# Four input places, solves on POOL and four-quadrant products in a recurrence with two feed-forward networks

## The chip, the cores and the metric

One core of one Trainium2 chip runs the program. Inputs are laid out by the host beforehand. The metric is the device time of one execution in microseconds (us).

## What is computed

The input has 4 batches x 8 heads (32 states), 768 steps and a head dimension of 40. Each head carries a 40 x 40 state:

```python
for t in range(S):
    y[:, :, t] = np.einsum('bhd,bhde->bhe', rt, state)
    Sa = np.einsum('bhde,bhe->bhd', state, at)
    state = state * wt[:, :, None, :] - np.einsum('bhd,bhe->bhde', Sa, bt) + np.einsum('bhd,bhe->bhde', vt, kt)
x = y.transpose(0, 2, 1, 3).reshape(B * S, H * D)   # 3072 x 320
h = x @ w_in                                         # 320 x 2048
g = np.where(h >= 1, h, np.where(h <= -1, 0.0, (h + 1) ** 2 / 4))
x = g @ w_out                                        # 2048 x 320
out = ((x @ w_a) * (x @ w_b)) @ w_out2               # 320 x 1536, 1536 x 320
```

The network weights arrive as 64-bit floats; the kernel turns them into 32-bit ones itself.

## The kernel before

**Chunks.** The 768 steps are cut into 24 chunks of 32; four chunks make a block. Within a chunk the recurrence is turned into small matrix products for each of the 32 states (16 pairs, two states of a pair on different partitions) and one triangular system per state.

**Preparation** (`prepare`, L118) of a chunk reads one 104 x 2065 tile, `ein`, loaded by `load_e` (L115). DVE scans the decays (L128, L131), POOL copies `wc` (L129) and sets `cre` (L127), DVE writes `lab` (L137), POOL scales k and b (L139; DVE for chunks 0 and 1), TensorE makes the products `pab` (L146, 64 columns each), and after them SP issues the next `ein` load into the same buffer. DVE masks the product into `lab` (L152), and ACT's queue writes a part of it, `amd`, to DRAM (L154). `p1_stage` (L158) does the same kind of scaling for a whole block (`ptw`, `pkb`, results `pwd` and `wtd` in DRAM).

**Solve.** The triangular systems are inverted by elimination on the whole block, 128 systems on 128 partitions: `solve` (L200) has 60 DVE instructions, each needing the one before (L209, L211). For the first block, `solve_pair` (L218) does two chunks at a time, with each system's rows split over two partitions, in 62 instructions (L236, L238), closed by a POOL selection (L241). The input `apm` is loaded from `amd`, the result goes to `xtd` in DRAM, and `load_xt` (L261) brings it back as `xtl`.

**The recurrence** (`core`, L284) of a chunk: `pw` (L295) multiplies `lab` and the state tile `ru`; ACT negates it into `ws` (L297); `pu` (L303) multiplies by the solved `xtl`; ACT copies it into `ru` (L306); `pss` (L314) gives the next state, which DVE scales (L317); then transposes `put` and `pst` (L325, L332). `outp` (L338) makes the outputs with `pg` (L344) and `py` (L355); `x_out` (L366) transposes them into `xa` for the first network. `pw` and `pu` write two quarters of 32 partitions each, 64 of 128 in all; `py` writes four quarters of 32.

**Order.** The program first drains preparations 0 and 1, the first solve, the first block stage, preparations 2 and 3, the second solve, and then all of `conv`, the conversion of the first network's weights, at a priority 300 places back. Then it walks through 26 slots. A slot g holds `core(g)`, `outp(g - 1)`, `x_out(g - 2)`, the preparations given to it (two a slot at first, then one), a share of the block stage and of the solve of a later block (the solve of block n in slots 4n - 2 and 4n - 1), and 16 steps of the first network (from slot 3 on) at a priority 8000 places back. A network block has 256 rows and takes some 33 steps, so half a block falls to a slot; what is left runs after the last slot. From slot 12 on the second network's weights are converted. A planner places instructions on each engine by priority and by its own costs, and each engine then works in that fixed order.

**Conversion.** `from_f64` (L489) uses four DVE instructions, two on ACT and one product on POOL for a tile, then ACT copies the high part and DVE or POOL subtracts (`SE`, two of three on DVE). `stage` gives one of two staging places; the loads are issued by SP.

**Networks.** The first network (`ffn1_half`, L616) has products `pha` and `ya`, DVE and ACT for the activation (L629 to L634), and POOL for the remainder `gl` (L636). The second (`Second`, L657) runs after all of it, block by block.

## Time and profile before

| what | us |
|---|---|
| median of 3 runs | 1578.63 |
| lowest, highest | 1574.61, 1583.82 |
| the profiled execution | 1573.97 |
| its span in the profile | 1572.3 |

Rows of a timeline give the start in us, the length in us, engine, line, operation, tiles and shapes, a count of like instructions that follow one another, and in brackets the idle time of the engine before them with what ended it. PE is TensorE's matmul, PEld its weight load, SPq the queue of SP. In the table by stretches each engine has its busy time and instructions, then come the granted TensorE clock as a share of full speed, the busy share of the 16 DMA engines, and their rate. TensorE's clock has two levels, 1.2 and 2.4 GHz; a share between 0.5 and 1 is a mean of both. A product of 32-bit floats stands as two matmul records.

### The profile page before, as it was taken

The numbers are of one execution on the slowest core, as the hardware profiler recorded it, in microseconds if no ns is written. First come the engines' busy times: TensorE is split into PE (matmuls) and PEld (weight loads), VectorE is DVE, ScalarE is ACT, GpSimd is POOL, SyncE is SP. The second block draws the span as 40 slices with busy tenths as digits, with TensorE's granted clock in tenths as the row PEclk, the third lists the DMA queues.
The fourth block names the chain that finished last, engine by engine and source line by source line (L and its number), as shares of the span: only waits on it lengthen the run. The fifth ranks groups of instructions, "written<-read, shape, count | busy, mean of one in ns | idle before, by whom it ended". The sixth has DMA issues, their size and how long they took to land.

```text
span 1572.3 us, 36942 instructions
## 1 busy us (share of the span) xinstructions
PE 1220.9 (78%) x15602; PEld 1099.9 (70%) x15602; DVE 829.0 (53%) x1690; ACT 537.3 (34%) x1193; POOL 473.7 (30%) x523
## 2 busy tenths in 40 slices
PE   0010233577798998988899998978999999999996
PEld 0010232566688887877789987877888888888885
DVE  6579587883584585458557737787421111111110
ACT  1213324123123333333343545666432222222221
POOL 7135433312112323221322223455422222222221
PEclk9999996556579878788899988999999999999999
DMA  5846677777534334343433334443110000100000
GB/s 131 185 106 159 127 154 161 169 151 158 123 101 113 93 83 108 96 104 94 114 93 87 105 102 126 129 141 100 41 49 21 18 20 18 37 1 17 1 18 19
DMA packets 193987, 144.34 MB, mean 92 GB/s; under 512 B 139028, under 2 KB 168724, under 8 KB 191316
## 3 DMA queue, kind: packets, MB, share of 16 engines
q1 hardware_dynamic: 168468, 138.74, 35.4%
q10 hardware_dynamic: 25344, 3.15, 1.5%
q8 instruction: 124, 2.03, 0.5%
q14 instruction: 51, 0.42, 0.1%
HBM read 111.97 MB, written 29.88 MB: 90 GB/s over the span
## 4 chain that ended last, share of the span: by engine, by line
PE 45%; DMA 6%; DVE 6%; issue 2%; ACT 1%; POOL 1%; SPq 0%; DVEq 0%; ACTq 0%; POOLq 0%
PE pb L582 9%; PE pa L582 7%; PE po L582 7%; PE ya L582 5%; PE pha L582 4%; DMA ein<-in_ein_dram 3%; PE pg L344 2%; PE ya L574 1%; PE pa L574 1%; PE pab L146 1%; PE pha L574 1%; PE pw L295 1%; PE pss L314 1%; PE pu L303 1%; PE put L325 1%
## 5 line engine op out<-in xcount | busy, mean ns | idle before, releaser
L636 POOL TENSOR_TENSOR gl<-cl,gh 128x256 fp32r<-128x256 f32 x192 | 152.5, 796 | 333.7 <-ACT gh L634 223.8
L683 DVE TENSOR_TENSOR gf<-pb,asb 128x512 f32<-128x512 f32 x72 | 49.8, 692 | 308.4 <-PE pb L582 308.4
L582 PE MATMUL pha<-xa,wi 128*128 128x256 f32 x1239 | 195.0, 301 | 0.0
L146 PE MATMUL pab<-lab,ein 40*64 40x32 f32 x1536 | 80.0, 259 | 143.0 <-POOL ein L139 75.9
L687 POOL TENSOR_TENSOR gl<-gf,gh 128x512 fp32r<-128x512 f32 x72 | 92.8, 1289 | 310.8 <-ACT gh L685 310.8
L582 PEld LDWEIGHTS pha<-xa,wi 128*128 128x128 f32 x1239 | 179.3, 211 | 0.0
L146 PEld LDWEIGHTS pab<-lab,ein 40*64 40x64 f32 x1536 | 71.0, 179 | 149.6 <-POOL ein L139 92.9
L582 PE MATMUL ya<-wo,gh 128*128 128x320 f32 x576 | 143.4, 331 | 5.1 <-ACT yo L892 5.1
L630 ACT ACTIVATE cl<-cl 128x256 f32<-128x256 f32 x192 | 80.1, 417 | 157.8 <-DVE cl L629 152.1
L502 POOL TENSOR_TENSOR cvf<-cvf,cve 128x256 f32<-128x256 f32 (+2 forms) x84 | 79.2, 943 | 128.3 <-DVE cve L500 74.4
L582 PE MATMUL ya<-wo,gl 128*128 128x320 f32 x384 | 115.0, 336 | 1.5 <-POOL gl L636 1.2
L303 PE MATMUL pu<-ws,xtl 32*32 32x40 f32 x1536 | 47.6, 226 | 83.2 <-DMA xtl<-xtd 72.2
L582 PEld LDWEIGHTS ya<-wo,gh 128*128 128x128 f32 x576 | 107.1, 208 | 5.9 <-ACT yo L892 5.6
L634 ACT CAST gh<-cl 128x256 fp32r<-128x256 f32 x192 | 77.6, 404 | 98.3 <-DVE cl L632 90.7
L582 PE MATMUL po<-wo,gh 128*128 128x320 f32 x504 | 108.5, 309 | 0.0
L629 DVE TENSOR_SCALAR cl<-pha 128x256 f32<-128x256 f32 x177 | 73.9, 417 | 62.5 <-PE pha L582 55.8
L303 PEld LDWEIGHTS pu<-ws,xtl 32*32 32x32 f32 x1536 | 40.9, 130 | 91.0 <-issue 76.5
L574 PE MATMUL pha<-xa,wi 128*128 128x256 f32 x177 | 61.1, 345 | 45.8 <-DVE cl L632 45.8
L632 DVE TENSOR_TENSOR cl<-pha,cl 128x256 f32<-128x256 f32 x177 | 74.1, 419 | 40.0 <-ACT cl L630 38.5
L685 ACT CAST gh<-gf 128x512 fp32r<-128x512 f32 x72 | 44.7, 620 | 138.2 <-DVE gf L683 138.2
L582 PE MATMUL pb<-wo,w 128*128 128x512 f32 x288 | 90.8, 397 | 0.0
L582 PE MATMUL pb<-wi,w 128*128 128x512 f32 x288 | 90.8, 396 | 0.0
(147 smaller groups left out, 2683.3 us busy)
## 6 DMA issues: line engine op xcount, KB each, us to landing
ein<-in_ein_dram SPq DMA_DIRECT2D x24, 838.9 KB
vut<-in_vtin_dram SPq DMA_DIRECT2D x24, 416.0 KB
raw<-in_moe_w_out_dram SPq DMA_DIRECT2D x28, 320.0 KB
pkb<-in_pin_dram SPq DMA_DIRECT2D x12, 640.0 KB
ru<-in_vin_dram SPq DMA_DIRECT2D x48, 160.0 KB
pwd<-pkb SPq DMA_DIRECT2D x12, 640.0 KB
kbi<-pwd SPq DMA_DIRECT2D x48, 160.0 KB
lg<-pwd SPq DMA_DIRECT2D x48, 160.0 KB
```

The costliest lines, as they stand in the source:

```text
L146: nc.tensor.matmul(pab[FR[p]:FR[p] + 64, j, :], lhsT=kb[o:o + D, j, :], rhs=lab[o:o + D, p, j, :], start=True, stop=True)
L303: nc.tensor.matmul(pu[UR[p]:UR[p] + C, j, :], lhsT=xt[o:o + C, hs.start + j, :], rhs=ws[o:o + C, hs.start + j, :], start=True, stop=True)
L502: nc.gpsimd.tensor_tensor(out=f, in0=f, in1=e.bitcast(F32), op=ALU.mult)
L574: nc.tensor.matmul(**products[0])
L582: nc.tensor.matmul(**p)
L629: nc.vector.tensor_scalar(out=cl, in0=ph, scalar1=-1.0, scalar2=1.0, op0=ALU.max, op1=ALU.min)
L630: nc.scalar.activation(out=cl, in_=cl, func=AF.Square, scale=0.5, bias=0.5)
L632: nc.vector.tensor_tensor(out=gf, in0=ph, in1=cl, op=ALU.max)
L634: nc.scalar.copy(out=gh, in_=gf)
L636: nc.gpsimd.tensor_tensor(out=gl, in0=gf, in1=gh.bitcast(F32), op=ALU.subtract)
L683: nc.vector.tensor_tensor(out=gf, in0=pb, in1=asb, op=ALU.mult)
L687: nc.gpsimd.tensor_tensor(out=gl, in0=gf, in1=gh.bitcast(F32), op=ALU.subtract)
```

## The change

It does these things:

- The inputs `ein` of chunks 0 to 3 get four places (three of them in tiles that later hold network weights); chunk 4 and later ones use the first place. All block-0 inputs of `p1_stage` get their own places too.
- Setting up memory: `cre`, `crp` are cleared by DVE, `kbi` is copied by ACT; the copy `wc` and the setting of `cre` move from POOL to DVE; the scaling of k and b moves to POOL for all but chunk 0, and that of `pkb` for the first block.
- `solve` runs on POOL instead of DVE. The first block's first half is solved on DVE, the second half on POOL, with its own tiles; both come after all four preparations.
- `pab` and `pg` are made in groups of 32 columns, two products in place of one of 64 columns. `pw` and `pu` write all four quarters of 32 partitions at once, in one bank instead of two; `ws` is one ACT instruction instead of two; `amd`, `xtd` and `xtl` have a layout for it, and `xtl` is one load on 128 partitions, with two tiles.
- The conversion of the first network's weights goes 900 places back instead of 300; its loads are issued by ACT; for the first 20 units there are six staging places instead of two (four of them in the two `xa` tiles). One of three subtractions is left on DVE (`SE`).

```diff
-            EIN = pre.tile([128, LE], F32, name="ein")
+            EIN = [pre.tile([128, LE], F32, name="ein")] + [spare(n, F32)[:, 0:LE] for n in ("wi3", "wo3", "wi2")]
...
-                nc.sync.dma_start(out=EIN[0:104], in_=ein[g])
+                nc.sync.dma_start(out=EIN[g if g < 4 else 0][0:104], in_=ein[g])
...
-                nc.gpsimd.memset(cr[:, 0:NEW - 1:SEG], 1.0)
+                nc.vector.memset(cr[:, 0:NEW - 1:SEG], 1.0)
...
-                nc.gpsimd.tensor_copy(out=wc, in_=wx[:, C::SEG])
+                nc.vector.tensor_copy(out=wc, in_=wx[:, C::SEG])
...
-                eng = nc.vector if g < 2 else nc.gpsimd
+                eng = nc.gpsimd if g else nc.vector
...
-                            nc.tensor.matmul(pab[FR[p]:FR[p] + 64, j, :], lhsT=kb[o:o + D, j, :],
-                                             rhs=lab[o:o + D, p, j, :], start=True, stop=True)
+                            for n in range(2):
+                                f = FR[p] + C * n
+                                nc.tensor.matmul(pab[f:f + C, j, :], lhsT=kb[o:o + D, j, n, :],
+                                                 rhs=lab[o:o + D, p, j, :], start=True, stop=True)
                     yield
-                if g + 1 < NCH:
+                if g == 0:
+                    load_e(4)
+                elif 4 <= g < NCH - 1:
                     load_e(g + 1)
...
-                    nc.vector.tensor_tensor(out=tv, in0=X[:, 0:m, m:m + 1].to_broadcast([128, m, n]),
+                    nc.gpsimd.tensor_tensor(out=tv, in0=X[:, 0:m, m:m + 1].to_broadcast([128, m, n]),
...
-                    nc.vector.tensor_tensor(out=X[:, 0:m, m + 1:], in0=X[:, 0:m, m + 1:], in1=tv, op=ALU.add)
+                    nc.gpsimd.tensor_tensor(out=X[:, 0:m, m + 1:], in0=X[:, 0:m, m + 1:], in1=tv, op=ALU.add)
...
-                    t = XT[g] = mid.tile([128, NC_, C], F32, name="xtl")
-                    for p in range(2):
-                        nc.sync.dma_start(out=t[XR[p]:XR[p] + C], in_=xtd[g // 4][g % 4, p].rearrange("k s t -> s k t"))
+                    t = XT[g] = mid.tile([128, HC, C], F32, name="xtl", bufs=2)
+                    nc.sync.dma_start(out=t, in_=xtd[g // 4][g % 4].rearrange("k q s t -> (q s) k t"))
...
+                quads = [(C * (2 * h + p), p, h) for h in range(2) for p in range(2)]
+                pw = bank("pw", [128, HC, D])
+                for j in range(HC):
+                    for q, p, h in quads:
+                        nc.tensor.matmul(pw[q:q + C, j, :], lhsT=lab[:, p, 2 * j + h, :],
+                                         rhs=ru[:, p, 2 * j + h, :], start=True, stop=True)
+                ws = mid.tile([128, HC, D], F32, name="ws")
+                nc.scalar.activation(out=ws, in_=pw, func=AF.Copy, scale=-1.0)
+                yield
+                pu = bank("pu", [128, HC, D])
+                for j in range(HC):
+                    for q, p, h in quads:
+                        nc.tensor.matmul(pu[q:q + C, j, :], lhsT=xt[q:q + C, j, :], rhs=ws[q:q + C, j, :],
+                                         start=True, stop=True)
+                for q, p, h in quads:
+                    nc.scalar.copy(out=ru[UR[p]:UR[p] + C, p, h::2], in_=pu[q:q + C])
...
             drain(prepare(0))
             drain(prepare(1))
-            drain(solve_pair(0))
             drain(p0)
+            drain(prepare(2))
+            drain(prepare(3))
+            drain(solve_pair(0, nc.vector))
             load_kb(0, KBI)
             load_kb(0, LG)
             load_wt(0)
-            drain(prepare(2))
-            drain(prepare(3))
-            drain(solve_pair(2))
-            with tc.high_priority(offset=-300):
-                for _ in conv:
-                    pass
+            drain(solve_pair(1, nc.gpsimd))
+            with tc.high_priority(offset=-900):
+                more = [xap.tile([128, 6, 256], F32R, name="xa").bitcast(U32).rearrange("p j t -> p (j t)") for _ in range(2)]
+                extra.extend(t[:, 640 * i:640 * i + 640].rearrange("p (n w) -> p n w", w=2) for t in more for i in range(2))
+                QS["raw"] = 'A'
+                for n, _ in enumerate(conv):
+                    if n == 20:
+                        extra.clear()
+                QS["raw"] = 'S'
...
-    SE = 'DDP'
+    SE = 'PPD'
```

## Rows read from the trace of the kernel before

**Rows 1.** Busy time by stretches (us from the span's start), all engines.
```profile
0.00:186.00 186.00, 16.78 (x320) 16.21 (x320) 126.19 (x226) 48.36 (x90) 84.40 (x84) 1.00 0.63 142
...
283.00:482.00 199.00, 151.84 (x2884) 136.69 (x2883) 138.08 (x245) 52.59 (x109) 40.73 (x43) 0.60 0.60 137
482.00:787.00 305.00, 269.73 (x4499) 246.24 (x4499) 188.70 (x408) 106.55 (x259) 83.41 (x108) 0.83 0.39 99
787.00:997.00 210.00, 198.83 (x3640) 182.87 (x3635) 129.50 (x311) 100.04 (x249) 60.66 (x86) 0.93 0.39 104
997.00:1122.00 125.00, 109.50 (x1172) 100.91 (x1167) 94.98 (x223) 77.37 (x199) 64.54 (x80) 1.00 0.37 107
1122.00:1572.00 450.00, 433.82 (x2293) 379.73 (x2291) 75.47 (x124) 119.85 (x222) 105.39 (x89) 0.99 0.07 22
```

**Rows 2.** Timeline of PE: products pu and pw of chunks 0, 4, 8, 16, 23.
```profile
186.51 0.44 PE L303 MATMUL pu<-ws,xtl 32*32 32x40 f32 x4 [66.70 <-DMA xtl<-xtd]
...
364.81 1.45 PE L303 MATMUL pu<-ws,xtl 32*32 32x40 f32 x27 [5.48 <-DMA xtl<-xtd]
...
483.41 0.77 PE L295 MATMUL pw<-ru,lab 128*32 128x40 f32 x32
...
786.70 0.77 PE L295 MATMUL pw<-ru,lab 128*32 128x40 f32 x32
...
996.44 0.77 PE L295 MATMUL pw<-ru,lab 128*32 128x40 f32 x32
```

**Rows 3.** Timeline of SP's queue, 60 to 180 us.
```profile
63.27 2.54 SPq L116 DMA_DIRECT2D ein<-in_ein_dram  x1
...
76.42 0.55 SPq L226 DMA_DIRECT2D apm<-amd  x1
...
163.86 5.02 SPq L244 DMA_DIRECT2D xtd<-apm  x2
...
172.19 4.74 SPq L265 DMA_DIRECT2D xtl<-xtd  x2
```

**Rows 4.** Timeline of DVE: first solve.
```profile
96.61 0.19 DVE L236 TENSOR_TENSOR tm<-apm 128x31 f32<-128x31 f32 x1 [9.35 <-POOL apm L230]
...
120.98 3.60 DVE L238 TENSOR_TENSOR apm<-apm,tm 128x126 f32<-128x126 f32 x1
```

**Rows 5.** Timeline of POOL beside it.
```profile
120.85 3.58 POOL L184 TENSOR_TENSOR pkb<-pkb,ptw 128x1280 f32<-128x1280 f32 x1 [1.09 <-DMA pkb<-in_pin_dram]
...
162.63 0.83 POOL L241 TENSOR_SCALAR_AFFINE_SELECT apm<-apm 128x512 f32<-128x512 f32 x1 [1.01 <-DVE apm L238]
```

**Rows 6.** Tile apm: count, ns min/median/max, first and last start, forms.
```profile
L209 DVE TENSOR_TENSOR tm<-apm x150: 166/368/3570, 298.9 to 883.5; 128x30 f32<-128x30 f32 x10, 128x58 f32<-128x58 f32 x10, 128x84 f32<-128x84 f32 x10, 128x108 f32<-128x108 f32 x10
...
L236 DVE TENSOR_TENSOR tm<-apm x62: 168/272/2536, 96.6 to 256.6; 128x126 f32<-128x126 f32 x6, 128x30 f32<-128x30 f32 x4, 128x56 f32<-128x56 f32 x4, 128x78 f32<-128x78 f32 x4
```

**Rows 7.** Groups by line and form on POOL: busy us, mean ns | idle before.
```profile
L636 POOL TENSOR_TENSOR gl<-cl,gh 128x256 fp32r<-128x256 f32 x192 | 152.5, 796 | 333.7 <-ACT gh L634 223.8 <-issue 59.3 <-PE pha L582 9.4
```

**Rows 8.** DMA from 0 to 482 us: total, and the loads of pkb.
```profile
DMA packets 122575, 69.12 MB, mean 143 GB/s; under 512 B 104907, under 2 KB 110923, under 8 KB 120971
...
pkb<-in_pin_dram SPq DMA_DIRECT2D x12, 640.0 KB
```

**Rows 9.** Timeline of PE: small products at either clock level.
```profile
682.22 0.80 PE L355 MATMUL py<-lg,rg 128*32 128x40 f32 x64
...
686.54 1.47 PE L146 MATMUL pab<-lab,ein 40*64 40x32 f32 x44
...
279.97 3.63 PE L146 MATMUL pab<-lab,ein 40*64 40x32 f32 x64 [16.12 <-DMA pkb<-in_pin_dram]
```

**Rows 10.** One wait for ein: chain of waits, then timelines of DVE and PE.
```profile
689.22 7.16 DMA ein<-in_ein_dram
...
696.41 1.26 DVE L128 TENSOR_TENSOR_SCAN ewx<-ein,cre 104x529 f32<-104x529 f32 x1 [5.02 <-DMA ein<-in_ein_dram]
...
698.04 0.58 PE L574 MATMUL pha<-xa,wi 128*128 128x256 f32 x1 [4.60 <-DVE cl L632]
```

More of the change, by code (lines that the diff above doesn't have):

```diff
@@ L42, in rwkv_moe_kernel @@
     wtd = [dram.tile([C, 4, NP // 2, 2, D], F32, name=f"wtd{i}") for i in range(NSB)]
-    amd = [dram.tile([4, 2, NP // 2, C, C], F32, name=f"amd{i}") for i in range(NSB)]
-    xtd = [dram.tile([4, 2, NP // 2, C, C], F32, name=f"xtd{i}") for i in range(NSB)]
+    amd, xtd = ([dram.tile([4, NP // 4, 4, C, C], F32, name=f"{n}{i}") for i in range(NSB)] for n in ("amd", "xtd"))
     const = ctx.enter_context(tc.tile_pool(name="const", bufs=1))
@@ L243, in solve_pair @@
                 for h in range(2):
-                    qu('xs').dma_start(out=xtd[sb][c:c + 2].rearrange("c p k (j h) t -> h (c p k) j t", h=2)[h, :, ::-1],
+                    nc.sync.dma_start(out=xtd[0][2 * i:2 * i + 2].rearrange("c k q (j h) t -> h (c k q) j t", h=2)[h, :, ::-1],
                                       in_=X[64 * h:64 * h + 64])
-                mark["solve", g] = last(DVE)
                 yield
@@ L286, in core @@
                 ru, nxt, lab, wc = RU[g % 2], RU[(g + 1) % 2], LAB[g % PL], WC[g % (PL + 1)]
[L287 removed]
+                if g % 4 == 0 or g == 2:
                     load_xt(g)
                 xt = XT.pop(g)
[L290 to L298 removed]
@@ L894, in ffn_block, with spare @@
             yield
-        step, conv2 = recurrence(ffn_block, wk, units1(stg, wa, WI, WO), lambda: units2(NE), early())
+        def spare(name, dtype):
+            return wa.tile([128, 2560], dtype, name=name)
+        step, conv2 = recurrence(ffn_block, wk, spare, units1(stg, wa, WI, WO), lambda: units2(NE), early())
         wo = w2s.enter_context(tc.tile_pool(name="wo2", bufs=1, side="right", reuse_waits="tile"))
```

103 lines of the change are left out of this document (46 added, 57 removed).

## The prediction

> **What bounds the kernel now.** I read the table by stages first, then followed the first late product backwards through the queues. In [rows 1] the last stage, 1122 to 1572, is TensorE at the higher clock level almost throughout (433.8 of 450 us, clock 0.99); the diff touches nothing there, so those 450 us stay. The first 186 us hold 16.8 us of TensorE work, with DVE at 126 us and the DMA engines at 0.63; from 283 to 482 TensorE runs at a mean clock of 0.60, that is mostly at 1.2 GHz. From 482 to 787 it is busy 270 of 305 us at 0.83. So there are two places to gain: the start, and the product stream between 283 and 997.
>
> The start is one chain. The first correction product (pu of chunk 0) begins at 186.51 after TensorE idled 66.70 us for the solved matrices [rows 2]. Backwards [rows 3 to 5]: xtl is loaded at 172.19, xtd written at 163.86, the solve's last step on POOL stands at 162.63, its first product on DVE at 96.61, its load (apm) was issued at 76.42, and at 63.27 the single ein buffer was only being filled for the third chunk. The solve took 66 us for 62 instructions whose median is 0.27 us [rows 6]: DVE did conversions and preparation between them, and was held by POOL, as at 120.98, where an addition of 126 elements took 3.60 us while POOL multiplied pkb for 3.58 us [rows 4, 5].
>
> The marks for pace are the starts of pu in chunks 0 and 4, 186.5 and 364.8, and of pw in chunks 8, 16 and 23, 483.4, 786.7 and 996.4 [rows 2]: some 37 us a chunk up to chunk 8, 38 from 8 to 16, 30 after that.
>
> **The front, up to chunk 8.** *Inputs.* With four places the loads of chunks 0 to 3 are issued at once. By the shapes, four ein are 4 x 104 x 2065 x 4 B = 3.4 MB, pin 2.0 MB, v, vt and r 1.2 MB, and six staged weight tiles about 1.7 MB on ACT's queue beside them: 8.3 MB, at the 142 GB/s of the first stage [rows 1] 58 us. The apm load of chunks 0 and 1 queues behind most of it, so its data are there at about 57 us, where now the first product starts at 96.6: 39 us earlier. *First solve.* 62 instructions at 0.27 us are 17 us [rows 6], now 66; chunks 2 and 3, the block scans and POOL's own second solve lie beside it, so I take 30, nearer the floor because conversions are put back by 900 places and not by 300. *From the last step to pu* it is 23.9 us now (162.63 to 186.51); one xtl load instead of two and a shorter SP queue, but the last step stands in POOL's queue among the second solve's: I take 20. Sum 57 + 30 + 20 = 107, so 80 us earlier; bounds 88 (57 + 17 + 14, the last from 172.19 on) and 147 (57 + 66 + 24).
>
> *Chunks 0 to 8.* Chunk 0 to 4 takes 178 us now. Its bound is the serial round of the one ein place (chunks 4 to 7 still use it), then the solve of the second block. The load of chunk 4 now starts early, which saves at most one round; the solve moves to POOL: 60 instructions of 30 to 240 elements. No row has POOL doing this. From below it costs DVE's 0.37 us each [rows 6], 22 us; from above the 0.80 us of POOL's 256-element subtraction [rows 7], 48 us. I take 0.6, 36 us, nearer that row because the largest steps have its size; DVE's row is stretched by conflicts too, so the chain is about even. I take 10 us less for chunks 0 to 4 and 5 less for 4 to 8 out of 119. Chunk 8 then starts at 107 + 168 + 114 = 389. *Can DMA follow?* By 482 us 69.1 MB have moved, all twelve pkb loads among them [rows 8], so the last three of six blocks (3 x 3.9 MB by shapes) are ahead of need: 57 MB are needed, at 142 GB/s 404 us. I take the gain at chunk 8 as 95 us (388); bounds 45 (the first solve's ceiling, and the rest unchanged) and 140 (its floor, with 42 us off the two stretches).
>
> **Small products.** py, 32 columns in four quadrants, takes 0.80 us for 64 records, 12.5 ns each; pw in two quadrants 0.77 us for 32, 24 ns [rows 2]; pab with 64 columns 1.47 for 44, 33 ns; at 1.2 GHz pab takes 3.63 for 64, 57 ns [rows 9]. A pw or pu of 64 records falls from 1.54 to 0.80 us, 0.74 less each; pab and pg double to 128 records but at 12.5 ns are 1.60 instead of 2.14, 0.54 less each. Sum 2.55 us a chunk at the higher level, about 1.7 times that, 4.4, at the lower (57 / 33). At the mean clock 0.83 of 482 to 787 a third of the time is at the lower level: 3.2 x 8 = 25 us; from chunk 16 on, mostly without pab (2.55 - 0.54, and a little at the lower level), 2.2 x 7 = 16. Sum 41. It counts only where TensorE is on the path. Every preparation still ends in a wait: the ein load takes 7.16 us, DVE's scan idles 5.02 us for it, TensorE then 4.60 us [rows 10], and nothing in the diff removes this after chunk 3. So the lower bound of this term is 0; the upper is 64, four us a chunk, if the clock falls less often.
>
> The Trainium skill, TensorE: Matmul & The Clock Gate, Part 3, says that a weight load runs beside matmuls in flight only when its row group differs. By that rule pw, with all 128 rows, would gain nothing from four column groups, and pab and pg would pay for twice the loads; py's row speaks against it. What this would make of the sum is the third rival.
>
> **Edits with little on the path.** *Solves of blocks 2 to 5 on POOL* add about 36 us each to a POOL that is busy 83 of 305 us; DVE loses 22. The subtraction gl of the first network waits behind one solve step at a time, under 1 us, and pab's multiplication on POOL too; DVE's two-input work is held meanwhile, as at 120.98. Taken as 0, bounds 20 gained and 30 lost. If POOL's cover went, chunk 4n would wait for xtl. *Weight loads on ACT*: 40 issues move from SP to ACT, which is 26% busy at the start; behind a load that waits for its staging place stand ws, the ru copies and the amd writes. Taken as 0, bounds 0 and 25 lost. *Memset of cre and copy wc on DVE*: under 0.5 us a chunk on an engine 62% busy, hidden by its waits for ein; without that cover 24 x 0.5 = 12 us. *Conversions later*: the weights wi1 to wi3, wo1, wo2 and wo3 are written only when chunks 1 to 3, the second solve and pkb have left their places, and the tile xa when staging is over. By 482 us little of the first network is done now either (2884 records from 283 on, where a chunk's recurrence has 451, two a product, and 5.6 chunks pass [rows 1, 2]), so this is covered; uncovered, the products it delays (half a network block a chunk) return in 997 to 1122, where TensorE is busy 110 of 125 us.
>
> **Sum.** The profiled execution took 1573.97 us, a span of 1572.3; it lies 0.3% under the median of 1578.63. 1574 - 95 - 41 = **1438 us**.
>
> **Rivals.** *Both halves pay in full* (0.14): 1574 - 140 - 64 = 1370. For it: the idle share of DMA at the start, and TensorE's 47 idle us with the lower clock in 283 to 482. Against: the ein round is kept. *The loads bound the front* (0.20): weights, four ein and the blocks compete, the first solve stays long, chunk 8 gains 45: 1574 - 45 - 41 = 1488. For it: 0.63 busy already with 142 GB/s. Against: three blocks' loads are not needed yet. *Column groups do not overlap* (0.05): pu alone gains 0.74, pab and pg cost 64 more records at 33 ns, 2.1 each: 3.5 lost in each of chunks 8 to 23, 56, so 1574 - 95 + 56 = 1535. Py's 12.5 ns against pw's 24 speaks against it. *Slower: the solve on POOL becomes the bound* (0.05). It has the two chunks before it is needed, some 64 us. Beyond that every microsecond holds chunk 4n, five times. At 2 us an instruction, 120 us, (120 - 64) x 5 = 280 are lost: 1574 - 136 + 280 = 1718. It decides the sign from (136 / 5 + 64) / 60 = 1.5 us an instruction; the row of 0.80 speaks against it.
>
> **The numbers.** The forecast has 0.52, with 1400 to 1475 of its own; 0.04 lies elsewhere, half of it within 0.5%, half slower. About 0.5%, 8 us, is what a measurement of this kernel can tell from none. The first three rivals are also faster: 0.91 faster, 0.02 same, 0.07 slower. The range reaches to both neighbours: 1365 to 1500 leaves out the third and fourth rival and the ends.
>
> **What would show it.** Right: pu of chunk 0 near 107, chunk 4 near 260, pw of chunk 8 near 388; pw and pu in four quadrants near 12.5 ns a record; steps of the solve on POOL at 0.4 to 0.8 us; the last stage unchanged at 450. Wrong: chunk 0 beyond 147, a long idle of pu at chunks 4, 8, 12 for xtl, pab beyond 2.1 us for 128 records, or the time between the end of the recurrence and the second network growing past 125 us.

## The result, and the profile after

The changed kernel takes 1521.51 us (median of 4 runs) where the kernel before, measured beside it, takes 1576.62: a ratio of 0.9657, 95% interval 0.9602 to 0.9713. The forecast was 1438, with a range of 1365 to 1500: the direction was right, the gain was 55 us instead of 136. The profiled execution has a span of 1521.4 us, 51 less than before. First its busy time by stretches, with the same columns as [rows 1] and cut at the starts of chunks 0, 4, 8, 16 and 23:

```profile
0.00:139.00 139.00, 9.00 (x580) 8.43 (x583) 100.72 (x173) 28.19 (x48) 75.48 (x105) 1.00 0.70 159
139.00:356.00 217.00, 98.35 (x2693) 86.90 (x2694) 154.84 (x238) 79.31 (x167) 142.34 (x147) 0.86 0.71 155
356.00:438.00 82.00, 58.99 (x2239) 51.43 (x2241) 36.38 (x64) 28.07 (x58) 39.20 (x57) 0.60 0.64 147
438.00:702.00 264.00, 220.74 (x5432) 200.13 (x5424) 135.28 (x262) 90.53 (x221) 133.68 (x215) 0.85 0.44 112
702.00:931.00 229.00, 190.28 (x4110) 173.27 (x4110) 123.59 (x287) 102.64 (x260) 97.87 (x156) 0.88 0.40 108
931.00:1071.00 140.00, 120.56 (x1352) 112.90 (x1349) 85.58 (x198) 76.74 (x197) 73.55 (x99) 0.89 0.31 93
1071.00:1521.00 450.00, 434.37 (x2298) 379.95 (x2296) 75.61 (x125) 120.31 (x223) 105.51 (x89) 0.99 0.07 22
```

The last stage is 450 us as before. From chunk 0 to chunk 4 it now takes 217 us (178 before) and POOL is busy for 142 of them. The rows below are to be compared with [rows 2] and [rows 9]; PE's timeline:

```profile
138.96 1.29 PE L303 MATMUL pu<-ws,xtl 32*32 32x40 f32 x64 [71.70 <-DMA xtl<-xtd]
...
356.40 0.78 PE L303 MATMUL pu<-ws,xtl 32*32 32x40 f32 x64
...
435.75 0.61 PE L295 MATMUL pw<-ru,lab 128*32 128x40 f32 x19
...
699.99 0.80 PE L295 MATMUL pw<-ru,lab 128*32 128x40 f32 x64
...
766.31 1.02 PE L146 MATMUL pab<-lab,ein 40*32 40x32 f32 x78
```

Chunk 0 starts 47.6 us earlier than in [rows 2], chunk 4 only 8.4, chunk 8 (pw) 47.7; of the 51 us only 3 were gained behind that. A pw of 64 records takes 0.80 us, 12.5 ns each, and a pab 13 ns a record. Where chunk 0's gain went is seen on SP's queue (to be compared with [rows 3]):

```profile
61.72 2.29 SPq L198 DMA_DIRECT2D wtd<-ptw  x2
64.10 2.63 SPq L168 DMA_DIRECT2D pkb<-in_pin_dram  x1
66.83 0.61 SPq L228 DMA_DIRECT2D apm<-amd  x1
...
125.86 2.56 SPq L247 DMA_DIRECT2D xtd<-apm  x2
...
251.99 0.34 SPq L206 DMA_DIRECT2D apm<-amd  x1
...
347.46 1.69 SPq L218 DMA_DIRECT2D xtd<-apm  x1
```

The second block's solve lies between the load of apm at 251.99 and the write of xtd at 347.46: 95 us on POOL, where DVE needed 59 before. The same two rows of the kernel before:

```profile
291.67 0.33 SPq L203 DMA_DIRECT2D apm<-amd  x1
...
350.52 2.25 SPq L215 DMA_DIRECT2D xtd<-apm  x1
```

The solve is loaded 40 us earlier and ends 3 earlier. What POOL does in that time, by groups (busy us, mean ns | idle us before them):

```profile
L214 POOL TENSOR_TENSOR apm<-apm,tm 128x30 f32<-128x30 f32 (+14 forms) x30 | 20.7, 690 | 1.4
L212 POOL TENSOR_TENSOR tm<-apm 128x30 f32<-128x30 f32 (+14 forms) x30 | 19.4, 645 | 1.5
L188 POOL TENSOR_TENSOR pkb<-pkb,ptw 128x1280 f32<-128x1280 f32 x3 | 10.8, 3596 | 2.8 <-DVE ptw L183 2.8
L512 POOL TENSOR_TENSOR cvf<-cvf,cve 128x256 f32<-128x256 f32 (+1 forms) x8 | 8.7, 1086 | 4.4 <-DVE cvf L511 4.4
L650 POOL TENSOR_TENSOR gl<-cl,gh 128x256 fp32r<-128x256 f32 x8 | 8.5, 1064 | 0.0
```

The solve's own 60 steps (L214 and L212) are 40 us. Between them stand later blocks' multiplications, the conversion, the first network's gl, and in three more groups (12 us) the scaling of kb and the conversion's subtractions: some 40 us together; the rest is mostly POOL's waits for their operands. POOL works in the order that the planner fixed, so each of them holds the next step. The steps themselves are about as short as forecast; the tile apm over the whole run (to be compared with [rows 6]):

```profile
L212 POOL TENSOR_TENSOR tm<-apm x150: 237/532/3131, 258.1 to 820.9; 128x30 f32<-128x30 f32 x10, 128x58 f32<-128x58 f32 x10, 128x84 f32<-128x84 f32 x10, 128x108 f32<-128x108 f32 x10
L214 POOL TENSOR_TENSOR apm<-apm,tm x150: 234/568/2889, 258.6 to 821.2; 128x30 f32<-128x30 f32 x10, 128x58 f32<-128x58 f32 x10, 128x84 f32<-128x84 f32 x10, 128x108 f32<-128x108 f32 x10
```

The first solve, on DVE, runs from 90.56 to 125.03 (66 us in [rows 4] and [rows 5], 34 now); its first and last steps on DVE's timeline:

```profile
90.56 0.18 DVE L239 TENSOR_TENSOR tm<-apm 128x31 f32<-128x31 f32 x1
...
124.84 0.19 DVE L241 TENSOR_TENSOR apm<-apm,tm 128x16 f32<-128x16 f32 x1
```

### The profile page after: what moved, and what is told of

It reads as the page before. It is cut to its first block, busy times and chain, and to the rows that moved or that the text cites. A ratio compares the mean times of both kernels' runs of the same rounds, so it can differ in the third digit from the quotient of the medians.

```text
span 1521.4 us, 43029 instructions
## 1 busy us (share of the span) xinstructions
PE 1132.3 (74%) x18674; PEld 1013.0 (67%) x18674; DVE 712.0 (47%) x1345; ACT 525.8 (35%) x1171; POOL 667.6 (44%) x866
## 4 chain that ended last, share of the span: by engine, by line
PE 52%; DMA 18%; DVE 12%; POOL 9%; issue 6%; ACT 2%; SPq 1%; ACTq 0%; POOLq 0%; DVEq 0%
PE pb L596 9%; PE pa L596 8%; PE po L596 8%; PE ya L596 7%; PE pha L596 6%; DMA ein<-in_ein_dram 6%; POOL apm L214 3%; POOL tm L212 2%; DMA ptw<-in_pin_dram 2%; DVE cve L510 2%; PE ya L588 2%; PE pss L314 1%; PE put L325 1%; DMA raw<-in_moe_w_b_dram 1%; DVE cvf L507 1%
## 5 line engine op out<-in xcount | busy, mean ns | idle before, releaser
L650 POOL TENSOR_TENSOR gl<-cl,gh 128x256 fp32r<-128x256 f32 x192 | 149.2, 781 | 196.8 <-ACT gh L648 126.9
L596 PE MATMUL pha<-xa,wi 128*128 128x256 f32 x1239 | 192.5, 299 | 0.0
L303 PE MATMUL pu<-ws,xtl 32*32 32x40 f32 x1536 | 28.0, 241 | 133.0 <-DMA xtl<-xtd 85.2
L512 POOL TENSOR_TENSOR cvf<-cvf,cve 128x256 f32<-128x256 f32 (+2 forms) x84 | 72.7, 869 | 113.8 <-DVE cvf L511 101.1
L303 PEld LDWEIGHTS pu<-ws,xtl 32*32 32x32 f32 x1536 | 23.9, 142 | 135.9 <-issue 95.9
L699 ACT CAST gh<-gf 128x512 fp32r<-128x512 f32 x72 | 44.7, 621 | 138.2 <-DVE gf L697 138.2
L136 POOL TENSOR_TENSOR ein<-ein 104x1024 f32<-104x1024 f32 x20 | 45.1, 2256 | 107.2 <-DVE ein L130 93.4
L695 ACT COPY asb<-pa 128x512 f32<-128x512 f32 x72 | 42.3, 587 | 138.0 <-PE pa L596 137.8
L214 POOL TENSOR_TENSOR apm<-apm,tm 128x30 f32<-128x30 f32 (+9 forms) x150 | 84.6, 564 | 8.8
```

The costliest lines, as they stand in the source:

```text
L136: eng.tensor_tensor(out=kb, in0=kb, in1=iw.unsqueeze(2).to_broadcast([104, NC_, 2, C]), op=ALU.mult)
L214: nc.gpsimd.tensor_tensor(out=X[:, 0:m, m + 1:], in0=X[:, 0:m, m + 1:], in1=tv, op=ALU.add)
L303: nc.tensor.matmul(pu[q:q + C, j, :], lhsT=xt[q:q + C, j, :], rhs=ws[q:q + C, j, :], start=True, stop=True)
L512: nc.gpsimd.tensor_tensor(out=f, in0=f, in1=e.bitcast(F32), op=ALU.mult)
L596: nc.tensor.matmul(**p)
L650: nc.gpsimd.tensor_tensor(out=gl, in0=gf, in1=gh.bitcast(F32), op=ALU.subtract)
```

## The experiments

The table has the start of pu in chunks 0, 4, 8 and 23 and of the second network (span less 450) from one profile of each kernel, in us, and the ratio to the kernel before measured beside it. Each kernel is the changed one with the edit named, where nothing else is said.

| kernel | chunk 0 | 4 | 8 | 23 | second network | ratio |
|---|---|---|---|---|---|---|
| before | 186.5 | 364.8 | 491.1 | 1003.6 | 1122.3 | 1 |
| changed | 139.0 | 356.4 | 454.1 | 936.7 | 1071.4 | 0.9657 |
| e1 solves on DVE | 139.9 | 341.3 | 448.3 | 952.5 | 1079.1 | 0.9684 |
| e2 before, products alone | 176.4 | 350.1 | 466.8 | 958.5 | 1077.4 | 0.9743 |
| e3 chunk 4 prepared early | 138.0 | 354.5 | 455.8 | 933.6 | 1058.9 | 0.9616 |
| e4 subtractions as before | 138.7 | 365.5 | 464.1 | 940.6 | 1071.8 | 0.9709 |
| e5 conversion at 300 places | 139.6 | 356.7 | 455.9 | 936.9 | 1066.5 | 0.9623 |
| e6 blocks after the solve | 140.1 | 315.9 | 464.8 | 934.5 | 1062.8 | 0.9547 |
| e7 e3, second solve on DVE | 138.2 | 332.4 | 443.8 | 935.6 | 1066.2 | 0.9578 |
| e8 staging as before | 135.4 | 370.3 | 464.0 | 963.9 | 1086.8 | 0.9750 |
| e9 e3 and e6 for all blocks | 138.9 | 308.8 | 425.0 | 936.0 | 1062.5 | 0.9613 |
| e10 e9, gl on DVE | 137.6 | 307.7 | 421.3 | 909.8 | 1034.9 | 0.9432 |
| e11 gl on DVE alone | 139.9 | 344.0 | 450.8 | 933.8 | 1056.5 | 0.9547 |
| e12 e10, apm early | 137.4 | 316.2 | 434.6 | 931.9 | 1057.2 | 0.9515 |
| e13 e10, cvf on DVE | 149.0 | 305.7 | 424.5 | 915.9 | 1041.7 | 0.9494 |
| e14 changed, conversion left out | 136.0 | 322.3 | 435.2 | 925.0 | 1050.0 | 0.9528 |
| e15 before, conversion left out | 157.9 | 334.6 | 452.4 | 963.3 | 1083.5 | 0.9708 |

The intervals are 0.4 to 0.9% to either side, so neighbours in the last column are not told apart by it alone.

**Products alone (e2).** The kernel before with the groups of `pab` and `pg`, the quarters of `pw` and `pu` and what goes with them (the layouts, one `ws` instruction, one `xtl` load) from the diff of the change, nothing else:

```diff
-                            nc.tensor.matmul(pab[FR[p]:FR[p] + 64, j, :], lhsT=kb[o:o + D, j, :],
...
+                                nc.tensor.matmul(pab[f:f + C, j, :], lhsT=kb[o:o + D, j, n, :],
...
+                    for q, p, h in quads:
+                        nc.tensor.matmul(pw[q:q + C, j, :], lhsT=lab[:, p, 2 * j + h, :],
```

> The kernel before with only the small products changed: pab and pg in 32-column groups, pw and pu in four quadrants, the amd and xtd layout and the single xtl load that these need; inputs, solves on DVE, conversions, queues and staging as before. My forecast's term: pu of chunk 0 about as before (186), 2.5 us a chunk less at the higher clock and 4.4 at the lower, 41 us less in chunks 8 to 23: 1574 - 41 = 1533. Theory P (that term is right, the front's part of the forecast failed): 1525 to 1545, and the changed kernel's front and its solves on POOL together are worth under 25 us net. Rival Q (preparation's waits hide the products, as the lower bound of that term had it): 1560 to 1580, and the 55 us gained by the whole change come from the front. Rival S (the products are worth all of it): under 1520, and everything else in the change is worth nothing or costs time.

1533.28 us, 40 under before (interval some 9 to either side): theory P, and the total that the forecast's term of 41 gave. Where it falls is not as forecast: chunk 0 is 10 us earlier and chunk 8 24, so that more than half of it lies before chunk 8. Everything else in the change then gives only some 12.

**Solves on DVE (e1).**

```diff
-                    nc.gpsimd.tensor_tensor(out=tv, in0=X[:, 0:m, m:m + 1].to_broadcast([128, m, n]),
+                    nc.vector.tensor_tensor(out=tv, in0=X[:, 0:m, m:m + 1].to_broadcast([128, m, n]),
...
-                    nc.gpsimd.tensor_tensor(out=X[:, 0:m, m + 1:], in0=X[:, 0:m, m + 1:], in1=tv, op=ALU.add)
+                    nc.vector.tensor_tensor(out=X[:, 0:m, m + 1:], in0=X[:, 0:m, m + 1:], in1=tv, op=ALU.add)
```

> The changed kernel with the solves of blocks 2 to 6 back on DVE (two operations in one loop), all else as changed; the first block's second half stays on POOL. Theory T (POOL's share is what holds chunk 4: there the second block's solve stood between its load at 252 us and its write at 347.5, 95 us, on POOL, which also had conversions and multiplications): the same stretch falls to about 60 us, as on DVE before, pu of chunk 4 starts near 325 instead of 356, and some 20 to 30 us of it are left at the end: 1490 to 1502 instead of 1521. Rival R (chunk 4 is late because its solve's inputs are late: the products pab of chunk 4 stand behind pu of chunk 0 in the order on TensorE, and the one input place turns four more times after that): the solve is still loaded near 250, DVE, which then also has preparation and conversions, needs 80 us or more, pu of chunk 4 starts within 10 us of 356 and the total is 1510 to 1530. On the stretch from chunk 16 to the end: if POOL's solves cost the tail, c16 to the second network falls from 370 to about 350.

1526.22 us. Chunk 4 is 15 us earlier, between the two theories, and nothing of it is left at the end. From pw of chunk 16 to the second network it takes 361 us, where the changed kernel takes 371: half of what was expected if POOL's solves cost that stretch. From SP's queue of this kernel:

```profile
252.55 0.34 SPq L206 DMA_DIRECT2D apm<-amd  x1
...
334.29 0.35 SPq L218 DMA_DIRECT2D xtd<-apm  x1
```

82 us now on DVE: on that engine, too, other work stands between the steps. Within the intervals, moving the solves to POOL neither gained nor lost.

**Chunk 4 prepared early (e3).**

```diff
             drain(prepare(3))
+            drain(prepare(4))
...
-                if g >= 4:
+                if g >= 5:
```

> The changed kernel with one move in the order: the preparation of chunk 4 (its scans, multiplications and pab) is issued right behind that of chunk 3, ahead of the recurrence of chunk 0. Nothing else changes. Rival R (the fixed order on TensorE holds pab of chunk 4, whose operands were ready at 69.6 us, behind pu of chunk 0 until 141, so that the one input place comes free for chunk 5 only at 157): the load of chunk 5 is issued some 60 to 80 us earlier, those of chunks 6 and 7 20 to 60 earlier, the load of the second block's solve falls from 252 to about 200 and pu of chunk 4 starts 30 to 50 us earlier, at 305 to 325, of which 20 to 45 us remain at the end: 1476 to 1501. Theory T (POOL is the bound of chunk 4): the solve is loaded earlier but POOL, which then has the same work in less time, ends it at about the same time, pu of chunk 4 within 15 us of 356, total 1505 to 1525.

1512.4 us. The place came free 70 us earlier (the next ein load is at 86.75 here, at 156.81 in the changed kernel), the solve was loaded 29 us earlier, and it ended 2 earlier:

```profile
86.75 0.43 SPq L115 DMA_DIRECT2D ein<-in_ein_dram  x1
...
222.79 0.33 SPq L206 DMA_DIRECT2D apm<-amd  x1
...
345.66 1.69 SPq L218 DMA_DIRECT2D xtd<-apm  x1
```

It took 123 us. So for chunk 4 rival R is out and T holds. The total is 9 us lower, but by the ratios the two kernels are not told apart.

**Subtractions as before (e4)**, `SE = 'DDP'` in place of `'PPD'`.

> The changed kernel with the subtractions of the weight conversion dealt out as before the change (two of three on DVE instead of one of three); it applies to the first network's weights at the start and the second's from chunk 12 on. Theory U (POOL, with solves and two of three subtractions, is what holds the second network's weights, and by that the stretch from chunk 16 to the second network, 35 us longer than before): that stretch falls from 370 by 10 to 25 us; the second block's solve on POOL falls from 95 us by up to 10; total 1495 to 1512. Rival V (the tail is longer only because less of the first network was done by then, work that was put back): the stretch stays within 6 us of 370, the total within 8 of 1521.

1526.67 us. From pu of chunk 16 to the second network it takes 347 us (724.9 to 1071.8) instead of 360 (711.9 to 1071.4), as theory U had it; but chunk 16 itself comes 13 us later, and the total is rival V's. What this sharing out gains in one stretch it loses in another.

**Conversion at 300 places (e5)**, `offset=-300` in place of `-900`.

> The changed kernel with the first network's conversion put back by 300 places, as before, and not by 900; loads on ACT, six staging places and all else as changed. Theory W (conversions put back pile up between chunk 0 and chunk 4, where the second block's solve and the blocks' multiplications also want POOL and DVE): pu of chunk 0 starts 10 to 30 us later than 139, conversions end earlier than 350, the second solve takes under 80 us, pu of chunk 4 starts earlier than 345 and the total is 1495 to 1512. Rival X (the vector engines' work up to chunk 4 is the same in any order): chunk 0 later, chunk 4 within 10 us of 356, total 1514 to 1530.

1520.46 us, chunks 0, 4, 8 and 23 within 2 us: rival X's total, but chunk 0 is not later. The number of places alone moves nothing here, so this run does not tell W from X.

**Blocks after the solve (e6).**

```diff
+                    with tc.issue_after(solved[1]) if sb > 1 else nullcontext():
-                    nc.gpsimd.tensor_tensor(out=kb[n], in0=kb[n], in1=iw, op=ALU.mult)
+                        nc.gpsimd.tensor_tensor(out=kb[n], in0=kb[n], in1=iw, op=ALU.mult)
```

`solved[1]` is the last POOL instruction of the second block's solve.

> The changed kernel with POOL's multiplications of the third and later blocks (pkb, 3.6 us each) issued behind the end of the second block's solve; the same work, in another order on POOL alone. In the changed kernel 26 other POOL instructions of some 40 us in all stood between the solve's steps. Theory T (these hold the solve, which is in order on one engine): the solve from its load to its write falls from 95 to 65 to 75 us, pu of chunk 4 from 356 to 325 to 335. If chunk 4 is on the path that sets the end, the total falls by 15 to 30: 1491 to 1506. Rival Y (the start of chunk 4 is not on that path, because TensorE fills the wait with the first network, as the run with the solves on DVE made it likely: chunk 4 15 us earlier and nothing gained): chunk 4 earlier as above and the total within 8 us of 1521, less than 15 us gained.

1509.89 us. The solve takes 65 us (241.97 to 307.27) instead of 95, and it is loaded 10 us earlier; chunk 4 starts at 315.9, 40 us earlier (theory T had 21 to 31). So work between the steps is what made chunk 4 late. But of 40 us the end keeps 12 by the medians and 17 by the ratios, between rival Y and theory T's lower end. POOL in the second solve, then in the third (369 to 455 us), by groups:

```profile
L217 POOL TENSOR_TENSOR apm<-apm,tm 128x30 f32<-128x30 f32 (+14 forms) x30 | 18.1, 603 | 1.9
L215 POOL TENSOR_TENSOR tm<-apm 128x30 f32<-128x30 f32 (+14 forms) x30 | 18.0, 602 | 1.8
...
L191 POOL TENSOR_TENSOR pkb<-pkb,ptw 128x1280 f32<-128x1280 f32 x1 | 3.6, 3569 | 0.0
...
L654 POOL TENSOR_TENSOR gl<-cl,gh 128x256 fp32r<-128x256 f32 x1 | 0.7, 722 | 0.0
```

```profile
L191 POOL TENSOR_TENSOR pkb<-pkb,ptw 128x1280 f32<-128x1280 f32 x3 | 11.1, 3690 | 14.4 <-DVE lab L138 14.4
L654 POOL TENSOR_TENSOR gl<-cl,gh 128x256 fp32r<-128x256 f32 x10 | 9.8, 988 | 11.5 <-ACT gh L652 11.5
```

In the second solve one pkb is left and one gl, beside 16 us of kb scaling and conversion; the third has three and ten, with 26 us of waits ahead of them, and takes 86 us instead of 45. The wait had moved from chunk 4 to chunk 8.

**Chunk 4 early and the second solve on DVE (e7)**: e3 with `nc.vector` in the solve of the second block.

> The changed kernel with two of the edits together: chunk 4 prepared right behind chunk 3, and the second block's solve on DVE (the later blocks' on POOL). Alone, the first gave 1512 with pu of chunk 4 at 354.5 (the solve loaded at 222.8 took 123 us on POOL), solves on DVE gave 1526 with chunk 4 at 341. Theory T (POOL's share held the earlier start back): loaded near 223, on DVE some 75 us, so pu of chunk 4 near 305 to 315, 40 to 50 earlier; if chunk 4 is on the path the total falls to 1475 to 1495. Rival Y (it is not on the path): chunk 4 as above, total 1505 to 1518, the gain of the first edit alone. Rival X (the vector work as a whole bounds the front, on whichever engine): chunk 4 not before 335.

1514.3 us, chunk 4 at 332.4: 24 us earlier, short of T's 305, and the solve took 97 us on DVE. Rival X is nearest: work that stands in front goes on either engine.

**Staging as before (e8)**: the block with `extra`, `xa` and ACT's queue in the diff above is replaced by the old one with 300 places.

> The changed kernel with its staging undone: the first network's weights are loaded by SP into two buffers and put back by 300 places, as before; four input places, solves on POOL and the products as changed. Theory Z (ACT's loads and the six buffers cost on the path what they bring: ws of chunk 2 stood 14 us behind ACT's queue): pu of chunk 2 starts earlier against chunk 0 than 111 us, total 1500 to 1515. Theory W (the later place of the conversions is what costs): as the run with 300 places alone, within 8 us of it. Rival V (staging is what lets the first solve have the engines to itself): pu of chunk 0 back beyond 165 instead of 139 and the total 1525 to 1540, about the products' gain alone.

1539.48 us. Staging is worth 15 us by the ratios, 18 by the medians. Since 300 instead of 900 places alone changed nothing (e5), that is ACT's queue or the six staging places, or both; these two were not tried apart. The total is rival V's, but not by its chunk 0, which was no later (135.4); chunk 4 was (370.3). Chunk 2 did come closer behind chunk 0, 100 us instead of 111 (234.9 less 135.4), as theory Z had it, and it did not count.

**All blocks after a solve (e9)**, e3 with e6's rule for `solved[sb - 1]`; **with gl on DVE (e10)**; **gl alone (e11)**.

```diff
-            nc.gpsimd.tensor_tensor(out=gl, in0=gf, in1=gh.bitcast(F32), op=ALU.subtract)
+            nc.vector.tensor_tensor(out=gl, in0=gf, in1=gh.bitcast(F32), op=ALU.subtract)
```

> The changed kernel with chunk 4 prepared right behind chunk 3, and POOL's multiplications of each block from the third on issued behind the end of the solve before it (block n behind solve n - 1). Theory T (what stands between a solve's steps in POOL's order holds the chunk that waits for it): in the run with the second rule for one solve only, the second solve took 65 us and the third 86 instead of 45; here the second is loaded near 225 and takes 60 to 75, pu of chunk 4 at 295 to 310, the third takes 40 to 60, pu of chunk 8 at 425 to 445. Rival Y (TensorE's own work, the first network beside the recurrence, sets the end once chunk 8 has begun, so that the start of chunk 23 stays at 935 as it did in five runs with chunk 8 between 444 and 465): total 1503 to 1515. If the earlier chunk 8 reaches the end: 1480 to 1500.

> The kernel of the run before this one, with the first network's subtraction gl on DVE instead of POOL (192 instructions of 0.73 us on POOL). Theory T: gl waits in POOL's order for ScalarE's gh, as at 401 to 409 us where it held a solve's step for 8 us; off POOL the solves run in one piece, some 45 us each, pu of chunk 8 10 to 20 us earlier than in that run; the total 5 to 15 us lower. Rival V (DVE, where pha's clips wait in turn, becomes later by the same): no gain, total within 6 us of that run or slower.

> The changed kernel with only gl moved from POOL to DVE. Theory T: seven gl stood between the steps of the second solve (some 8 us of POOL's time in 225 to 347), so the second solve falls from 95 by 5 to 15 us and pu of chunk 4 from 356 to 342 to 351; the later solves, 45 to 58 us, by 5 to 10 each; total 1508 to 1517. Rival V (DVE loses what POOL gains): total 1519 to 1535.

e9: 1518.86 us. The second solve took 85 us, still among conversions, the third 52; chunks 4 and 8 came 48 and 29 us earlier, and chunk 23 at 936.0 all the same, as rival Y said (the total is 4 us above its range). e10: 1488.57 us, the best, 30 under e9, twice the most that was expected. The solves stayed at 82 and 52 us and chunk 8 came only 4 us earlier, so T's mechanism is not what paid: the gain lies after chunk 8. e11: 1508.58 us and chunk 4 at 344.0, as T had it, with most of the gain behind chunk 23. The groups of gl from chunk 8 to 23, of e9 and of e10:

```profile
L655 POOL TENSOR_TENSOR gl<-cl,gh 128x256 fp32r<-128x256 f32 x112 | 87.3, 783 | 167.0 <-ACT gh L653 105.0 <-issue 38.5 <-PE pha L601 5.5
```

```profile
L655 DVE TENSOR_TENSOR gl<-cl,gh 128x256 fp32r<-128x256 f32 x111 | 61.0, 552 | 25.8 <-ACT gh L653 23.4 <-PE pst L336 0.5
```

On POOL the engine stands idle 167 us before a gl in that stretch, and solve steps, kb and pkb stand behind it; on DVE 26. TensorE itself is idle 104 us in that stretch in e9 and 78 in e10; only 12 and 5 us of that are direct waits for gl, so by which waits the rest was saved is not shown.

**The first solve's load ahead (e12)**, on e10.

```diff
             drain(prepare(1))
-            drain(p0)
+            sp0 = solve_pair(0, nc.vector)
+            next(sp0)
+            with tc.issue_after(last(SP)):
+                drain(p0)
```

> The fastest kernel so far (chunk 4 prepared early, blocks' multiplications behind the solve before them, gl on DVE; 1488.6, pu of chunk 0 at 137.6, of chunk 4 at 307.7) with one more move: on SP's queue the first solve's load apm goes ahead of the first block's writes pwd and wtd and the next load of pkb, in front of which it stood. Theory Q (in the changed kernel chunk 1's matrices were written at 57.5 us, but apm was issued at 66.8 behind wtd, which waits for ScalarE's copy, and its data were there at 90.3, 23 us later, among the block's transfers): issued near 58, data at 72 to 80, pu of chunk 0 10 to 18 us earlier, at 120 to 128. If the start of chunk 0 reaches the end: total 1471 to 1482. Rival Y (chunk 4's solve and what follows do not depend on it): pu of chunk 4 within 5 us of 308, total within 6 us of 1488.6.

1507.25 us, slower than e10. Theory Q was right for the load and wrong for chunk 0. Rival Y was wrong too: chunk 4 came 9 us later (316.2), and the total is 19 us above e10's. SP's row, then the first and last steps on DVE's timeline:

```profile
59.13 0.61 SPq L232 DMA_DIRECT2D apm<-amd  x1
```

```profile
74.83 0.18 DVE L243 TENSOR_TENSOR tm<-apm 128x31 f32<-128x31 f32 x1
...
128.61 0.19 DVE L245 TENSOR_TENSOR apm<-apm,tm 128x16 f32<-128x16 f32 x1
```

In e10 the solve runs from 89.21 to 129.86. So the data came 14 us earlier, the solve took 54 us instead of 41, and chunk 0 starts at 137.4 instead of 137.6. In e8 it was the same: 70.2 to 121.9, 52 us where the changed kernel needs 34. DVE is busy 43 of the 54 us, the 62 steps of the solve being 23 of them; the rest is other work.

**cvf on DVE (e13)**, on e10: `nc.vector` for the last product of `from_f64`.

> The same fastest kernel so far, with the conversion's multiplication (cvf, 40 instructions of 0.75 to 0.9 us on POOL) on DVE. There the second solve takes 82 us, from 216.6 to 298.4; 35 us of it are its own steps, 12 cvf with 9.9 us of waiting for DVE ahead of them, nine subtractions of the conversion, three multiplications of kb. Theory T (the exchange between DVE and POOL, in order on both, holds it): the solve falls to 58 to 70 us, pu of chunk 4 to 285 to 300, total 1475 to 1488. Rival V (DVE, 122 of 170 us busy between chunks 0 and 4, is the later one then: the conversions, and with them the solve and the first network, wait for it): chunk 4 at 305 or later, total 1488 to 1505.

1499.89 us; the second solve 76 us, chunk 4 2 us earlier, chunk 0 11 later: rival V. By the ratios the loss against e10 is not clear of the intervals.

**Conversion left out (e14, e15)**, in the changed kernel and in the kernel before: the arithmetic is left out for the first network, so these kernels compute with other weights and stand here for their time alone.

```diff
+        if plain[0]:
+            nc.scalar.activation(out=f, in_=hi, func=AF.Copy, scale=2.0 ** -40)
+            return f
```

> The changed kernel with the conversion's arithmetic left out for the first network: each tile of weights is loaded as before and only scaled once by ScalarE, in place of four instructions on DVE, two on ScalarE and one on POOL; the later subtraction stays. The computed weights are therefore others. Theory T (what DVE and POOL do in their fixed order up to a solve's last step sets its end, and the 40 conversions, some 3.6 us of DVE each with waits, are the largest part that is not needed there): the first solve takes 20 to 28 us instead of 34, pu of chunk 0 starts at 120 to 132 instead of 139, the second solve takes 55 to 75 instead of 95, pu of chunk 4 at 295 to 325 instead of 356; total 1490 to 1505. Rival R (the rounds through the one input place hold chunk 4): chunk 4 within 15 us of 356 and the total within 10 of 1521.

> The kernel before with the same arithmetic left out. Theory T: the first solve, which took 66 us from its first product, takes 30 to 45, pu of chunk 0 at 150 to 168 instead of 186.5, pu of chunk 4 at 315 to 340 instead of 365; total 1540 to 1560. If the changed front is worth more once conversions are out of its way, the pair without them lies further apart than 55 us: 55 to 75. Rival R: before gains the same as the changed kernel or more, the pair 40 to 55 apart.

1502.81 and 1532.89 us. Theory T for the solves: the second takes 63 us and chunk 4 starts at 322.3; before, chunk 0 starts at 157.9. Chunk 0 of the changed kernel, at 136.0, is a miss: the solve still took 31 us, its last step on DVE was done at 116.6, and the selection that closes it then waited 4 us behind pkb. POOL's timeline of e14:

```profile
116.85 3.52 POOL L188 TENSOR_TENSOR pkb<-pkb,ptw 128x1280 f32<-128x1280 f32 x1 [1.71 <-DMA pkb<-in_pin_dram]
...
120.68 0.72 POOL L244 TENSOR_SCALAR_AFFINE_SELECT apm<-apm 128x512 f32<-128x512 f32 x1
```

The total of e15 is below theory T's range. The pair lies 30 us apart, less even than rival R's 40 to 55: the kernel before gains more by leaving the conversion out. So a part of what the change is worth is that it hides the conversion better; by which of its edits is not shown.

**Once more, with five and more runs of each, side by side (e16 to e18):** e10, the changed kernel and e2, unaltered.

> The fastest version (chunk 4 prepared early, blocks' multiplications behind the solve before them, gl on DVE), over five rounds: 1485 to 1498, 25 to 35 us under the changed kernel of the same call.

> The changed kernel as it is, over five rounds: 1518 to 1526, a ratio of 0.962 to 0.969 to the kernel before.

> The small products alone, over five rounds: if the rest of the change is worth what the first calls gave, 10 to 15 us above the changed kernel, 1530 to 1537; if it is worth nothing, within 5 us of it.

1485.19 us (ratio 0.9443, interval 0.9402 to 0.9485), 1517.62 (0.9663, 0.9621 to 0.9705) and 1531.55 (0.9746, 0.9706 to 0.9786), before 1571.65. So the products alone are worth 40 us and all the rest of the change 14 on top of them; e10's three edits beat the changed kernel by 32 us and the kernel before by 86.

## Why the prediction was wrong, step by step

Of the 83 us that the forecast missed, 48 lie before chunk 8 (436 instead of 388) and some 36 behind it.

- *Data of the first solve at 57 us, solve 30, tail 20, chunk 0 at 107.* Measured: 90.6, 34, 14, 139.0, inside the bounds of 88 to 147. The first term counted bytes only. The write of chunk 1's part was issued at 56.3 us, but apm stood on SP behind wtd, which waits for ScalarE, until 66.8, and its data took 23 us more; before, too, 20 us lay between the issue at 76.42 and the first product at 96.61 [rows 3, 4]. The row was there and I did not add it. And e12 shows that the term was not one to be summed: data 14 us earlier made the solve 13 us longer.
- *Chunk 0 to 4 in 168 us: the step that failed.* It took 217. I let what chunk 0 gains pass through to chunk 8, with the stretches behind it a little shorter, and put the second block's solve on POOL at 36 us, "about even" with DVE. The solve's own steps were sized well: medians of 532 and 568 ns for the forecast's 0.6. What lay between them was not sized at all. The serial round of the one ein place, which the forecast took as the bound, was not it: freed 70 us earlier, it moved the solve's end by 2 (e3). Chunk 4 waits for a solve whose end is set by all that POOL (or DVE, in e1 and e7) has in its order up to there; that work did not shrink. In the changed kernel its end moved by 3 us while its load moved by 40.
- *Chunk 4 to 8 in 114 us:* 79. While chunk 4 waited, TensorE did network products that it otherwise did between chunks 4 and 8: 8 records of pha fall there now, 104 did before. The first network's products pha, counted up to pu of chunks 4 and 8 (window, TensorE's busy time on them, records; then clock and DMA), before and changed:

```profile
0.00:364.80 364.80, 3.78 (x16) 0.85 0.69 152
0.00:491.10 491.10, 22.33 (x120) 0.81 0.64 142
```

```profile
0.00:356.40 356.40, 19.22 (x120) 0.91 0.71 156
0.00:454.10 454.10, 20.33 (x128) 0.84 0.69 153
```

- *95 us at chunk 8:* 47.7 by pw. By pu, which at chunk 8 now waits 13.5 us for xtl, 37 us, of which the products alone give 24 (e2). The forecast let the 41 us of the products fall after chunk 8 only; more than half of them fell before it, inside the gain that I had given to the front. The rest of the change brought 13 us to pu of chunk 8 (26 to pw). The forecast's own sum of bytes gave 404 us for chunk 8, later than the 388 that it took.
- *Products 41 us, after chunk 8: the second step that failed.* Their total is 40 in both measurements, and that it agrees is in part luck, because the forecast had all of it behind chunk 8. There the stages show something else ([rows 1] from 482 us, the table by stretches at the start of this part from 438): up to chunk 23 TensorE's busy time fell from 469 to 411 us, more than forecast, but its idle time rose from 46 to 82 us, among it 14 for ACT's `lg` and 13 each for `ws` and for chunk 8's xtl. The condition was in the forecast (it counts only where TensorE is on the path), and its central value left it out. The rates were as read from py: 12.5 ns for pw, and pab 13. The third rival is out. The Trainium skill, TensorE: Matmul & The Clock Gate, Part 3, has weight loads overlap with products in flight only when their row groups differ; pw has all 128 rows in every record and fell from 24 to 12.5 ns by four column groups, so for this the measurement decides.
- *Solves on POOL, 0 (bounds 20 gained, 30 lost):* 5 us gained in e1, inside the runs' spread. Right in size.
- *Weight loads on ACT, taken as 0, up to 25 lost:* with them and the six staging places undone (e8) the kernel is 15 to 18 us slower, so together they gain. What ACT's queue does alone is not shown.
- *Conversions later, covered:* as far as the number of places goes, yes: 300 instead of 900 changed nothing (e5). The conversions themselves were not off the path: without their arithmetic the changed kernel gains 19 us and the kernel before 45, which no term of the sum priced.
- *The tail,* pu of chunk 23 to the second network, grew from 118.7 to 134.7 us (130.4 in e17, the same kernel); with gl off POOL it is 122.7 (e11). The same rows show what grew, from 997 us in [rows 1] and from 931 here: TensorE's granted clock is 0.89, a mean of its two levels, instead of 1.00, all at 2.4 GHz (it had been idle 82 of 493 us ahead of this stretch, and 46 of 515 before), and its busy time 121 us instead of 110, its idle time 19 instead of 16. At the same clock that busy time would be no longer (an estimate: 0.89 x 120.6 is 107). I had named the tail as a sign of a wrong forecast and put no price on it.
- The second rival (1488) had about the measured gain at chunk 8, 45 us, by luck: its reason, a first solve that stays long, did not come true (34 us), and it had the products once more behind chunk 8. The slower rival, POOL's solve as the bound, had the right place and the wrong form: the steps' medians stayed under 0.6 us, and it was other work between them that made it 95 us.

What stays open in part: why an earlier chunk 4 or 8 does not reach chunk 23. It starts at 932 to 937 us in eight kernels with chunk 4 between 309 and 357. In all eight TensorE is busy 578 to 594 us up to there, and 1032 to 1048 of the 1418 pha records stand before it; where chunk 4 is early, these products move behind it (e6 has 48 pha records before chunk 4 and 176 before chunk 8). So the wait for chunk 4 was not lost to TensorE as a whole. In e9 chunks 8 to 23 lengthen by 28 us against the changed kernel; with gl on DVE as well (e10) they take 488 and chunk 23 comes at 910, while gl alone (e11) leaves it at 934. Which wait it is in each was not settled. That e12 loses 19 us against e10 by a small change in order (e13 11, which is not clear of the intervals) shows how far such an order can swing.

## What to carry to other kernels

When a serial chain runs on an engine with a fixed order, price what the planner will put between its steps, not the steps: list every instruction of that engine in the stretch, and ask whether an earlier start only makes the chain longer. A gain early in a chain counts at the end only if the next thing waited for does not have its own supply of work; and a term that saves time everywhere must not be counted again inside a stage that is forecast as a whole. An instruction that waits for a third engine (gl for ScalarE) is worth trying on another queue than such a chain's: here this gained 13 us alone by the medians (e11) and 30 with the chain's order mended (e10), though the chain itself became hardly shorter.

## What the runs showed of the hardware

DVE held by POOL was known from [rows 4, 5]. The other way round was new to me: POOL is held by DVE's scans. From the changed kernel, DVE's timeline, then POOL's:

```profile
331.48 2.90 DVE L178 TENSOR_TENSOR_SCAN pwx<-ptw,crp 128x1321 f32<-128x1321 f32 x1
...
336.19 2.91 DVE L183 TENSOR_TENSOR_SCAN ptw<-ptw,crp 128x1321 f32<-128x1321 f32 x1
```

```profile
331.51 3.39 POOL L650 TENSOR_TENSOR gl<-cl,gh 128x256 fp32r<-128x256 f32 x1
...
336.41 2.89 POOL L214 TENSOR_TENSOR apm<-apm,tm 128x108 f32<-128x108 f32 x1
```

A gl takes 0.74 us elsewhere in that timeline, this step about 0.4. The Trainium skill, SBUF — State Buffer, "SBUF: two separate sides", says that the two engines share a pair of ports, which whoever starts first holds for its whole instruction, a DVE operation with two inputs in SBUF among them when the POOL operation reads SBUF; these rows agree. So moving work from DVE to POOL does not make it free of DVE's long instructions.
